# A kernel's last dense layer by seven block products instead of eight

## The chip, the core and the metric

One core of a Trainium2 chip runs the kernel. Its engines are TensorE (PE, with its weight loads as PEld), VectorE (DVE), ScalarE (ACT), GpSimd (POOL) and SyncE (SP, which here only issues DMAs). Time is device microseconds (us) for one execution.

## What is computed

Three blocks follow each other: attention with a decaying mask, a gated convolution between two dense layers, and a Fourier mix with a two-layer perceptron. The last part, cut to what the change touches (2304 tokens, 512 features, 2048 inner features):

```python
X = np.fft.fft(x, axis=1)
X = np.fft.fft(X, axis=2)
u = x + np.real(X)
mu = np.mean(u, axis=-1, keepdims=True)
var = np.mean((u - mu) ** 2, axis=-1, keepdims=True)
un = (u - mu) / np.sqrt(var + 1e-06)
ch = np.maximum(un @ w_ch1, 0.0) @ w_ch2
return u + ch
```

Inputs are float32, but the weights come as float64 and are decoded on the chip. Matmuls run on a rounded 32-bit type; every operand is split into a high and a low part, and each product is made of three matmuls (high by high, low by high, high by low; `HL` in line 46).

## The kernel before

The program records every operation with its tiles. A planner then orders them: it knows a cost for each operation and a lag between engines, walks the graph from the back for priorities and from the front for the order, and keeps the best of 40 rounds (`Plan.order`). Every engine then runs its own list strictly in order. So an edit of the recorded operations changes the lists of all engines, also far from the edit.

Up to about 460 us the lists hold attention, the gated convolution (`b_chunk`, `c_chunk`) and most of the Fourier stage (`dft`). In their gaps the weights of 7 of the 16 feature blocks (NST, 128 inner features each) are decoded (`fetch_ch`: an ACT, a POOL and three DVE operations) and put aside in DRAM; the other nine are decoded in the last stage.

The last stage is the two dense layers. Tokens go in chunks of 512, 512, 512, 512 and 256 (`chunks`, line 1081). For a chunk, `prep_u` reads the centred rows from DRAM, transposes them and splits them into high and low, into one half of `u_all` (name bc_wi in the trace), so that two chunks have room. For a chunk and a feature block:

- `ch1` (line 1110): 12 matmuls (4 slices of 128 features, three each) with 512 token columns into one of two PSUM banks (psc_c__4737 and psc_c__4738). ACT writes relu as the high part, and DVE's SCALAR_TENSOR_TENSOR the low part (bc_xs).
- `ch2` (line 1137), one block behind: for each 128 tokens three matmuls of 512 columns into an accumulator bank that stays open over all the blocks of a pass. Six banks rotate (psc_c__4989 to 4992, psdft_x__3932 and 3933).

Chunks 0 and 1 take their 16 blocks in two passes of 8, the others in one (`passes`). After the last block of a pass a 128-token tile is scaled by its 1/sqrt(var + 1e-6), computed by nine small DVE operations for each tile (`rsqrt`), added to its u row and stored. While the first passes run, the last pieces of the Fourier stage (`gens[3]`) are put between.

## Time and profile before

| | us |
|---|---|
| median of 3 runs | 866.22 (864.75 to 867.55) |
| the profiled execution's own time | 865.78 |
| its span, first to last instruction | 864.0 |
| PE busy in the span | 835.4 (97%), 5148 matmuls |
| DVE busy | 519.0 (60%) |
| ACT busy | 374.6 (43%) |
| POOL busy | 221.7 (26%) |
| mean granted clock of TensorE | 0.993 of 2.4 GHz |

Busy time of PE is that of overlapping, pipelined matmuls: the mean duration of one (some 390 ns for 512 columns) is longer than the step from one to the next. The step is read from the chain of waits, where twelve matmuls in a row have one entry. All names that begin with psc_c are PSUM banks of the last stage; a line number of 513 or 511 is that of the helper that issues every operation, so tiles tell more than lines.

### The profile page before, as it was taken

How to read it: one execution, taken by the hardware profiler on the slowest of the kernel's cores; microseconds unless marked ns; L12 is line 12 of the kernel's file. 1: busy time of each engine (PE TensorE's matmuls, PEld its weight loads, DVE VectorE, ACT ScalarE, POOL GpSimd, SP SyncE). 2: the span in 40 equal slices, each digit the busy share in tenths (PEclk: the TensorE clock that was granted, in tenths of full speed). 3: DMA queues.
4: the chain of work that ended last, by engine and by line, in shares of the span. 5: the costliest groups of instructions: out<-in, count | busy, mean ns of one | idle time of the engine just before them, and what ended most of it. 6: DMA issues, size and time to landing. Idle time of an engine off the chain costs nothing.

```text
span 864.0 us, 14103 instructions
## 1 busy us (share of the span) xinstructions
PE 835.4 (97%) x5148; PEld 703.4 (81%) x5148; DVE 519.0 (60%) x1364; ACT 374.6 (43%) x906; POOL 221.7 (26%) x252
## 2 busy tenths in 40 slices
PE   8988999899989999998999999999999999999998
PEld 6666887599878898997987888888888888888897
DVE  6978899856997374187586888676353113411141
ACT  5987798835756463274344443332121111110111
POOL 2243435401351042278465522220000000000000
PEclk9999999999999999999999999999999999999999
DMA  6454465899437414784998385433121001100110
GB/s 222 151 202 144 139 221 167 280 302 316 136 118 250 146 30 115 240 280 121 269 242 204 112 209 164 151 121 98 50 73 49 1 1 49 50 1 1 48 50 25
DMA packets 75269, 119.86 MB, mean 139 GB/s; under 512 B 10392, under 2 KB 44984, under 8 KB 75200
## 3 DMA queue, kind: packets, MB, share of 16 engines
q1 hardware_dynamic: 74624, 116.01, 44.2%
q0 software_dynamic: 576, 2.95, 1.0%
q8 instruction: 40, 0.66, 0.3%
q14 instruction: 29, 0.24, 0.1%
HBM read 93.66 MB, written 27.70 MB: 140 GB/s over the span
## 4 chain that ended last, share of the span: by engine, by line
PE 51%; DMA 4%; POOL 3%; DVE 2%; ACT 1%; issue 1%; SPq 0%; DVEq 0%; POOLq 0%; ACTq 0%
PE psc_c__4738 L513 11%; PE psc_c__4737 L513 11%; PE psc_c__4989 L513 5%; PE psc_c__4990 L513 4%; PE psdft_x__3933 L513 4%; PE psdft_x__3932 L513 4%; PE psc_c__4991 L513 3%; PE psc_c__4992 L513 3%; PE psbc_bc__537 L513 2%; PE psbc_bc__538 L513 2%; DMA dft_zz__3771<-dram_t__348 1%; POOL dft_t__3766 L513 1%; DMA dram_t__350<-glu_t__140 1%; DVE glu_cv__158 L513 1%; PE psatt_u__174 L505 1%
## 5 line engine op out<-in xcount | busy, mean ns | idle before, releaser
L513 DVE SCALAR_TENSOR_TENSOR bc_xs__131<-psc_c__4738,bc_xs__131 128x512 fp32r<-128x512 f32 (+1 forms) x40 | 25.5, 637 | 100.1 <-ACT bc_xs__131 L513 100.1
L513 DVE SCALAR_TENSOR_TENSOR bc_xs__131<-psc_c__4737,bc_xs__131 128x512 fp32r<-128x512 f32 (+1 forms) x40 | 25.4, 636 | 100.2 <-ACT bc_xs__131 L513 100.1
L513 ACT ACTIVATE bc_xs__131<-psc_c__4738 128x512 fp32r<-128x512 f32 (+1 forms) x40 | 22.2, 556 | 133.3 <-PE psc_c__4738 L513 129.2
L513 ACT ACTIVATE bc_xs__131<-psc_c__4737 128x512 fp32r<-128x512 f32 (+1 forms) x40 | 22.3, 557 | 129.6 <-PE psc_c__4737 L513 128.9
L513 PE MATMUL psbc_bc__538<-bc_xs__131,bc_wi__130 128*128 128x288 f32 x384 | 62.1, 299 | 0.0
L513 PE MATMUL psbc_bc__537<-bc_xs__131,bc_wi__130 128*128 128x288 f32 x384 | 61.7, 300 | 0.2 <-ACT glu_t__138 L513 0.2
L513 PEld LDWEIGHTS psbc_bc__537<-bc_xs__131,bc_wi__130 128*128 128x128 f32 x384 | 53.4, 188 | 1.5 <-issue 0.5
L513 PEld LDWEIGHTS psbc_bc__538<-bc_xs__131,bc_wi__130 128*128 128x128 f32 x384 | 54.0, 188 | 0.7 <-issue 0.7
L513 DVE SCALAR_TENSOR_TENSOR glu_cv__157<-glu_t__138,bc_t__132,glu_cv__157 128x576 f32<-128x576 f32 x32 | 34.4, 1076 | 12.4 <-ACT glu_cv__157 L513 12.1
L513 POOL TENSOR_SCALAR wprep_dw__125<-wprep_dw__125 128x512 f32<-128x512 f32 x24 | 16.1, 672 | 71.3 <-ACT wprep_dw__125 L513 71.0
L513 DVE SCALAR_TENSOR_TENSOR glu_cv__158<-glu_t__139,bc_t__132,glu_cv__158 128x576 f32<-128x576 f32 x32 | 32.0, 999 | 3.5 <-ACT glu_cv__158 L513 3.3
L513 DVE COPY glu_t__140<-psbc_bc__538 128x256 f32<-128x256 f32 (+2 forms) x48 | 10.0, 260 | 30.2 <-PE psbc_bc__538 L513 29.0
L513 POOL TENSOR_SCALAR wprep_dw__122<-wprep_dw__122 128x512 f32<-128x512 f32 x24 | 15.8, 656 | 43.9 <-ACT wprep_dw__122 L513 43.8
L505 PE MATMUL psatt_s__171<-att_t__67,att_t__66 64*128 64x288 f32 (+2 forms) x48 | 26.5, 553 | 0.3 <-DVE att_t__67 L513 0.3
L505 PE MATMUL psatt_s__170<-att_t__67,att_t__66 64*128 64x288 f32 (+2 forms) x48 | 26.3, 549 | 0.0
L505 PE MATMUL psatt_u__174<-att_pt__101,att_tv__92 128*64 128x448 f32 (+3 forms) x80 | 21.6, 417 | 0.6 <-ACT att_pt__102 L513 0.5
L505 PE MATMUL psatt_u__174<-att_pt__102,att_tv__93 128*64 128x448 f32 (+3 forms) x80 | 21.6, 417 | 0.0
L505 PE MATMUL psatt_s__172<-att_t__67,att_t__66 64*128 64x288 f32 (+2 forms) x48 | 21.5, 454 | 0.0
L505 PE MATMUL psatt_s__173<-att_t__67,att_t__66 64*128 64x288 f32 (+2 forms) x48 | 21.3, 449 | 0.0
L505 PE MATMUL psatt_u__169<-att_pt__101,att_tv__99 128*64 128x448 f32 (+4 forms) x72 | 19.4, 415 | 1.6 <-ACT att_pt__102 L513 1.6
L505 PE MATMUL psatt_s__170<-att_qk__70 64*128 64x288 f32 (+2 forms) x48 | 18.8, 476 | 1.8 <-DVE att_nb__95 L513 1.8
L513 DVE SCALAR_TENSOR_TENSOR wprep_dw__125<-wprep_dr__124,wprep_dw__125 128x512 int32<-128x512 int32 x24 | 20.1, 837 | 0.2
(721 smaller groups left out, 2703.1 us busy)
## 6 DMA issues: line engine op xcount, KB each, us to landing
bc_wo__133<-dram_t__346 SPq DMA_DIRECT2D x16, 512.0 KB
wprep_dr__124<-in_moe_w_ch_dram SPq DMA_DIRECT2D x16, 512.0 KB
wprep_dr__121<-in_moe_w_ch_dram SPq DMA_DIRECT2D x16, 512.0 KB
bc_wo__134<-dram_t__346 SPq DMA_DIRECT2D x16, 512.0 KB
att_qk__70<-in_qk_dram SPq DMA_DIRECT2D x8, 608.0 KB
att_qk__91<-in_qk_dram SPq DMA_DIRECT2D x8, 608.0 KB
att_rb__68<-dram_t__345 SPq DMA_DIRECT2D x32, 144.0 KB
wprep_dr__124<-in_moe_w_out_dram SPq DMA_DIRECT2D x8, 512.0 KB
```

Source lines behind the costliest of these rows:

```text
L505: getattr(eng[op.eng], f)(**{k: v.real() if isinstance(v, View) else v for k, v in kw.items()})
L513: getattr(eng[op.eng], op.fn)(**kw)
```

## The change

The first dense layer is no longer computed block by block. Two feature blocks (a pair), two halves of the 512 input features and two halves of a chunk's tokens make a 2 by 2 by 2 block product, and that is formed from seven products instead of eight: sums and differences of the blocks of the weights (`load_pair`) and of the rows (`prep_u`) are multiplied, and the seven results are added up in seven VectorE additions (`ch1`). One product is 6 matmuls with half a chunk's columns. Chunks are 512, 512, 640 and 640 tokens, so the products have 256 or 320 columns. All chunks take their 8 pairs in two passes; the first three pairs of chunks 0 and 1 are still computed the plain way. The first pass of a chunk is scaled by ACT and stored to DRAM (`y_d`), and the second adds it. `u_all` now holds one chunk (seven operands of the rows), so it is rebuilt in place at five changes of chunk. NST is 10, the weights of the last six blocks are decoded in the third and fourth pass, and `rsqrt` works on all tiles of a chunk at once.

```diff
 NH = B * H
 NT = B * S
 NP = NH // 2
-NWO, NST, NUC = 2, 7, 2
-NZT, NZR, NPQ, NUN = 1, 1, 0, 2
+NWO, NST = 2, 10
+NZT, NZR, NPQ, NUN, NUS = 1, 1, 0, 2, 1
 NZS = 1
-CUTS = (0, 8, 16)
-NMR, G3 = 7, (2, 2)
-ULE, W2E = 'V', 'V'
+G3 = 3
 NCV, NZZ, NZO, NX = 2, 4, 2, 5
 NUO, NWARM = 1, 10
 LASTW = 256
...
+    chunks = [(0, 512), (512, 512), (1024, 640), (1664, 640)]
+    passes = [(0, (0, 1, 2)), (1, (0, 1, 2)), (2, (0, 1, 2, 3, 4)), (3, (0, 1, 2, 3, 4)),
+              (3, (5, 6, 7)), (2, (5, 6, 7)), (1, (3, 4, 5, 6, 7)), (0, (3, 4, 5, 6, 7))]
+    u_all = shared[0]
-    chunks = [(512 * i, 512) for i in range(4)] + [(2048, 256)]
-    passes = [(i, range(a, z)) for a, z in zip(CUTS, CUTS[1:]) for i in (0, 1)] + [(i, range(NFC)) for i in (2, 3, 4)]
...
+    def load_pair(q, k):
+        p, w = slots[k]
+        plain = q < 3
+        wa, wb = stored(0, 2 * q), stored(0, 2 * q + 1)
+        s12, s4 = (wp.tile([128, 512], F32, tag="de", bufs=2) for _ in range(2))
+        V.tensor_tensor(out=s12[:, 0:256], in0=wb[:, 0:256], in1=wb[:, 256:512], op=ALU.add)
+        V.tensor_tensor(out=s12[:, 256:512], in0=s12[:, 0:256], in1=wa[:, 0:256], op=ALU.subtract)
+        V.tensor_tensor(out=wb[:, 0:256], in0=wa[:, 0:256], in1=wb[:, 0:256], op=ALU.subtract)
+        V.tensor_tensor(out=s4[:, 0:256], in0=wa[:, 256:512], in1=s12[:, 256:512], op=ALU.subtract)
+        if plain:
+            hi(p[1][:, 0, 0], wb[:, 0:256])
+            lo(G, p[1][:, 0, 1], wb[:, 0:256], p[1][:, 0, 0])
+        for dst, src in zip(p, (wa, wb, s12)):
+            if plain and src is not s12:
+                continue
+            hi(dst[:, :, 0], src.group(2))
+            lo(G, dst[:, :, 1], src.group(2), dst[:, :, 0])
+        hi(p[3][:, 0], s4[:, 0:256])
+        lo(G, p[3][:, 1], s4[:, 0:256], p[3][:, 0])
+        for x in range(0 if plain else 2):
+            t = stored(1, 2 * q + x)
+            hi(w[x][:, 0], t)
+            lo(V, w[x][:, 1], t, w[x][:, 0])
+
+    def u_op(n, k, j, x):
+        h = n // 2
+        if n > 512 and k == 6:
+            return u_last.over(2 * h * j + h * x, [1, h])
+        return u_all.over(4 * h * k + 2 * h * j + h * x, [1, h])
...
+    def prep_u(ci, uc):
         n = chunks[ci][1]
-        ps = ps_c1.tile([128, 512], F32, tag="c1", bufs=2)
-        k = 0
-        for d in range(4):
-            for wx, ux in HL:
-                mm(ps[:, 0:n], w1[fo][:, wx, 128 * d:128 * d + 128], U[ux][d][:, 0:n], k == 0, k == 11)
...
+        h = n // 2
+
+        def both(k, j, src):
+            up, dn = (u_op(n, k, j, x) for x in range(2))
+            hi(up, src)
+            lo(V, dn, src, up)
+
+        def wide(k, j, src):
+            up, dn = (u_all.over(4 * h * k + 2 * h * j + h * x, [4 * h, 2], [1, h]) for x in range(2))
+            hi(up, src[:, 0:n].group(2))
+            lo(V, dn, src[:, 0:n].group(2), up)
+
+        for j in range(2):
+            both(0, j, uc[j][:, 0:h])
+        for j in range(2):
+            wide(2, j, uc[j + 2])
+        for j in range(2):
+            b1, b2 = uc[j], uc[j + 2]
+            t12 = ml.tile([128, 640], F32, tag="ta")
+            V.tensor_tensor(out=t12[:, 0:h], in0=b1[:, h:n], in1=b1[:, 0:h], op=ALU.subtract)
+            V.tensor_tensor(out=t12[:, h:n], in0=b2[:, h:n], in1=t12[:, 0:h], op=ALU.subtract)
+            V.tensor_tensor(out=b1[:, h:n], in0=b2[:, h:n], in1=b1[:, h:n], op=ALU.subtract)
+            V.tensor_tensor(out=b2[:, 0:h], in0=b2[:, 0:h], in1=t12[:, h:n], op=ALU.subtract)
+            wide(4, j, t12)
+            both(1, j, b1[:, h:n])
...
+    def ch1(ci, k):
+        n = chunks[ci][1]
+        h = n // 2
+        p = slots[k][0]
+        ga_, gb_ = g_tile(n), g_tile(n)
+        a, c, d, e = (tmp.over(320 * i, [1, h]) for i in range(4))
+
+        def product(w, k):
+            ps = ps_c1.tile([128, 512], F32, tag="c1", bufs=2)[:, 0:h]
+            i = 0
+            for j in range(2):
+                for wx, ux in HL:
+                    mm(ps, w[:, wx, 128 * j:128 * j + 128], u_op(n, k, j, ux), i == 0, i == 5)
+                    i += 1
+            return ps
+
+        def gated(g, c0, v):
+            split(g[:, 0, c0:c0 + h], g[:, 1, c0:c0 + h], v)
+
+        def plus(o, ps, v):
+            V.tensor_tensor(out=o, in0=ps, in1=v, op=ALU.add)
+
+        A.activation(out=a, in_=product(p[0][:, 0], 0), func=AF.Copy)
+        plus(e, product(p[0][:, 1], 2), a)
+        gated(ga_, 0, e)
+        plus(c, product(p[2][:, 1], 5), a)
+        plus(d, product(p[1][:, 0], 1), c)
+        x = product(p[2][:, 0], 4)
+        plus(c, x, c)
+        plus(a, x, d)
+        gated(gb_, h, a)
+        plus(d, product(p[1][:, 1], 6), d)
+        gated(gb_, 0, d)
+        plus(c, product(p[3], 3), c)
+        gated(ga_, h, c)
+        return ga_, gb_
+
...
+    def ch2(step):
+        ci, k, gs, acc, first, last, final, end = step
         t0, n = chunks[ci]
-        gh, gl = g_
-        first, last = fo == fos[0], fo == fos[-1]
+        if last:
...
+            for f in range(2):
+                g, w = gs[f], slots[k][1][f]
+                for i, (gx, wx) in enumerate(HL):
+                    mm(acc[t], g[:, wx, 128 * t:128 * t + 128], w[:, gx], first and f == 0 and i == 0, last and f == 1 and i == 2)
             if last:
                 r = t0 + 128 * t
-                ut = ml.tile([128, 514], F32, tag="ut", bufs=2)
-                dma(out=ut, in_=Flat(u_d, UW * r, [UW, 128], [1, UW]))
-                rstd = rsqrt(ut[:, 513:514])
-                if fo == NFC - 1:
-                    V.tensor_scalar(out=ut[:, 0:512], in0=ut[:, 0:512], scalar1=ut[:, 512:513], scalar2=None, op0=ALU.add)
-                cols = 512 if ci + 1 < len(chunks) else LASTW
+                if not final:
+                    ut = mr.tile([128, 512], F32, tag="us", bufs=NUS)
+                    A.activation(out=ut, in_=acc[t], func=AF.Copy, scale=rstd[:, t:t + 1])
+                    dma(out=y_d[r:r + 128], in_=ut)
+                    continue
+                ut, yt = wp.tile([128, 512], F32, tag="dw", bufs=2), ml.tile([128, 512], F32, tag="yt", bufs=1)
+                dma(out=ut, in_=Flat(u_d, UW * r, [UW, 128], [1, DM]))
+                dma(out=yt, in_=y_d[r:r + 128])
+                V.scalar_tensor_tensor(out=ut, in0=ut, scalar=st[:, t, 0:1], in1=yt, op0=ALU.add, op1=ALU.add)
+                cols = LASTW if end else 512
                 for c in range(0, 512, cols):
                     o = ut[:, c:c + cols]
-                    V.scalar_tensor_tensor(out=o, in0=acc[t][:, c:c + cols], scalar=rstd, in1=o,
+                    V.scalar_tensor_tensor(out=o, in0=acc[t][:, c:c + cols], scalar=rstd[:, t:t + 1], in1=o,
                                            op0=ALU.mult, op1=ALU.add)
-                    dma(out=out[r:r + 128, c:c + cols] if fo == NFC - 1 else Flat(u_d, UW * r + c, [UW, 128], [1, cols]), in_=o)
-
-    pend = None
-    for k, (ci, fos) in enumerate(passes):
-        if ci not in us:
-            us[ci] = prep_u(ci)
-        acc = {}
-        for fo in fos:
-            for _ in range(G3[k] if k < len(G3) else 0):
-                next(gens[3], None)
-            if fo not in w1:
-                w1[fo] = load_ch(0, fo, G)
-                w2[fo] = load_ch(1, fo, G if W2E == 'G' else V)
-            g_ = ch1(ci, fo, us[ci])
-            if pend:
-                ch2(*pend)
-            pend = (ci, fos, fo, g_, acc)
-    ch2(*pend)
+                    dma(out=out[r:r + 128, c:c + cols], in_=o)
...
+    todo = [(w, fo) for fo in range(NST, NFC) for w in range(2)]
+
+    def decode_some(m):
+        for _ in range(m):
+            if todo:
+                w, fo = todo.pop(0)
+                dma(out=wch_d[2 * fo + w], in_=fetch_ch(w, fo))
+
+    pend, acc, home = None, {}, {}
+    prep_plain(0)
+    load_plain(0, 0)
+    prep_plain(1)
+    flat = [(i, ci, q) for i, (ci, qs) in enumerate(passes) for q in qs]
+    for i, (pi, ci, q) in enumerate(flat):
+        qs = passes[pi][1]
+        if q == qs[0]:
+            acc = {}
+            if pi in (2, 3, 5, 6, 7):
+                prep_u(ci, turned)
+            if pi in (2, 4, 5, 6):
+                turned = turn_u(passes[pi + 1][0])
+        for _ in range(G3):
+            next(gens[3], None)
+        k = q % 5
+        if pi == 0 and q < 2:
+            load_plain(q + 1, q + 1)
+        gs = plain_ch1(ci, k) if pi < 2 else ch1(ci, k)
+        if pend:
+            ch2(pend)
+        pend = (ci, k, gs, acc, q == qs[0], q == qs[-1], pi > 3, pi + 1 == len(passes))
+        if pi == 1:
+            load_pair(q, k)
+            if q == qs[0]:
+                turned = turn_u(2)
+        if pi == 2:
+            decode_some(2)
+            if q < 2:
+                load_pair(q + 3, q + 3)
+        if pi == 3:
+            decode_some(2)
+            if 0 < q < 4:
+                load_pair(q + 4, q - 1)
+    ch2(pend)
```

TensorE, well inside the last stage. Before, one feature block of a 512-token chunk (psc_c_0__4737 is the first layer's bank, the four names after it are accumulators of the second layer):

```order
L513 MATMUL psc_c_0__4737<-bc_wi__130,ml_t_0__5271 128x512 x12
L513 MATMUL psc_c_0__4989<-ml_t_0__5270,bc_xs__131 128x512 x3
L513 MATMUL psc_c_0__4990<-ml_t_0__5270,bc_xs__131 128x512 x3
L513 MATMUL psc_c_0__4991<-ml_t_0__5270,bc_xs__131 128x512 x3
L513 MATMUL psc_c_0__4992<-ml_t_0__5270,bc_xs__131 128x512 x3
L513 MATMUL psc_c_1__4738<-bc_wi__130,ml_t_0__5273 128x512 x12
```

Now a pair of a 640-token chunk from its first product on (psc_c_0__4873 and psc_c_1__4874 are the first layer's two banks, ml_t_0__5372 to 5375 the weight sums of the pair, the rest accumulators):

```order
L511 MATMUL psc_c_0__4873<-bc_wi__130,ml_t_0__5372 128x320 x6
L511 MATMUL psc_c_1__4874<-bc_wi__130,ml_t_0__5372 128x320 x6
L511 MATMUL psdft_x__3869<-mr_t_0__4899,ml_t_0__5371 128x512 x3
L511 MATMUL psc_c_0__4873<-bc_wi__130,ml_t_0__5374 128x320 x6
L511 MATMUL psc_c_0__5045<-mr_t_0__4904,bc_xs__131 128x512
L511 MATMUL psc_c_1__4874<-bc_wi__130,ml_t_0__5373 128x320 x6
L511 MATMUL psc_c_0__5045<-mr_t_0__4904,bc_xs__131 128x512 x2
L511 MATMUL psc_c_0__4873<-bc_wi__130,ml_t_0__5374 128x320 x6
L511 MATMUL psc_c_0__5045<-mr_t_0__4905,bc_xs__131 128x512
L511 MATMUL psc_c_1__4874<-ml_t_0__5370,ml_t_0__5373 128x320 x6
L511 MATMUL psc_c_0__5045<-mr_t_0__4905,bc_xs__131 128x512 x2
L511 MATMUL psc_c_0__5046<-mr_t_0__4904,bc_xs__131 128x512
```

A bank used to be filled by 12 long matmuls and then left alone for 12 of the second layer; it is now filled by 6 shorter ones, and the other bank's next product follows at once or after one to three matmuls of the second layer.

TensorE at the change from chunk 2 to chunk 3 in the changed kernel. The rows on ml_t_0__5379 to 5381 are the old chunk's last products (ml_t_0__5370 and bc_wi__130 hold the rows' operands), that on bc_xs__131 with 128x320 the new chunk's first:

```order
L511 MATMUL psc_c_1__4874<-ml_t_0__5370,ml_t_0__5379 128x320 x6
L511 MATMUL psc_c_0__5044<-ml_t_0__5377,bc_xs__131 128x512 x2
L511 MATMUL psc_c_0__5046<-ml_t_0__5382,bc_xs__131 128x512 x3
L511 MATMUL psc_c_0__5047<-ml_t_0__5382,bc_xs__131 128x512
L511 MATMUL psc_c_0__4873<-bc_wi__130,ml_t_0__5381 128x320 x6
L511 MATMUL psc_c_0__5047<-ml_t_0__5382,bc_xs__131 128x512 x2
L511 MATMUL psc_c_1__4874<-bc_wi__130,bc_xs__131 128x320 x6
L511 MATMUL psc_c_0__5046<-ml_t_0__5383,ml_t_0__5371 128x512 x2
L511 MATMUL psc_c_0__5047<-ml_t_0__5383,ml_t_0__5371 128x512 x2
L511 MATMUL psc_c_0__5046<-ml_t_0__5383,ml_t_0__5371 128x512
L511 MATMUL psc_c_0__5047<-ml_t_0__5383,ml_t_0__5371 128x512
L511 MATMUL psc_c_1__4874<-bc_wi__130,mr_t_0__4892 128x320 x3
```

Between the old chunk's last product (the fifth row) and the new chunk's first (the seventh) stand two matmuls of the second layer. Before, the next chunk's rows had a half of bc_wi of their own.

VectorE, in the same part of the program. Before, at the change from one chunk to the next (the rows on wprep_de and bc_wi build the next chunk's rows, those on psc_c_0__4737 and psc_c_1__4738 empty the first layer's banks, those on ml_ut finish an output tile):

```order
L513 STREAM_TRANSPOSE wprep_de__123<-bc_xs__131 128x512
L513 TENSOR_TENSOR bc_wi__130<-wprep_de__126,bc_wi__130 128x512
L513 TENSOR_TENSOR bc_wi__130<-wprep_de__123,bc_wi__130 128x512
L513 SCALAR_TENSOR_TENSOR bc_xs__131<-psc_c_0__4737,bc_xs__131 128x512
L513 SCALAR_TENSOR_TENSOR ml_ut__5255<-psc_c_0__4991,ml_rs_0__5256,ml_ut__5255 128x512
L513 SCALAR_TENSOR_TENSOR ml_ut__5259<-psc_c_0__4992,ml_rs_1__5260,ml_ut__5259 128x512
L513 STREAM_TRANSPOSE wprep_de__126<-bc_xs__131 128x512
L513 SCALAR_TENSOR_TENSOR bc_xs__131<-psc_c_1__4738,bc_xs__131 128x512
```

Now, in the first pass of a 640-token chunk (ml_t_0__5369 holds the partial sums, wprep_dw, de and dr the decoding of a weight block):

```order
L511 TENSOR_SCALAR wprep_de__126<-wprep_dw__125 128x512
L511 TENSOR_TENSOR ml_t_0__5369<-psc_c_0__4873,ml_t_0__5369 128x320
L511 SCALAR_TENSOR_TENSOR wprep_dw__125<-wprep_dr__124,wprep_de__126 128x512
L511 TENSOR_SCALAR wprep_de__123<-wprep_dw__122 128x512
L511 SCALAR_TENSOR_TENSOR ml_t_0__5371<-ml_t_0__5369,ml_t_0__5371 128x320
L511 SCALAR_TENSOR_TENSOR wprep_dw__122<-wprep_dr__121,wprep_de__123 128x512
L511 SCALAR_TENSOR_TENSOR bc_xs__131<-ml_t_0__5369,bc_xs__131 128x320
L511 SCALAR_TENSOR_TENSOR wprep_dw__122<-wprep_dr__121,wprep_dw__122 128x512
L511 SCALAR_TENSOR_TENSOR wprep_dw__125<-wprep_dr__124,wprep_dw__125 128x512
L511 TENSOR_TENSOR ml_t_0__5369<-psc_c_0__4873,ml_t_0__5369 128x320
L511 TENSOR_TENSOR ml_t_0__5369<-psc_c_1__4874,ml_t_0__5369 128x320
```

A product's result is now added by a VectorE operation that stands in one list with the decoding of weights: here five decoding operations of 512 elements and two low parts of 320 lie between two additions that read the same bank.

## Rows read from the trace of the kernel before

**Rows 1.** The page: span and part 1, busy us, share of span, instructions.

```profile
span 864.0 us, 14103 instructions
...
PE 835.4 (97%) x5148; PEld 703.4 (81%) x5148; DVE 519.0 (60%) x1364; ACT 374.6 (43%) x906; POOL 221.7 (26%) x252
```

**Rows 2.** Busy time by stretch (us): PE, PEld, DVE, ACT, POOL, PEclk, DMA, GB/s.

```profile
0.00:460.00 460.00, 436.38 (x3299) 374.01 (x3300) 336.99 (x866) 288.54 (x756) 179.90 (x197) 0.99 0.63 195
460.00:864.00 404.00, 399.00 (x1851) 329.39 (x1849) 182.02 (x500) 86.08 (x150) 41.78 (x55) 1.00 0.26 75
...
480.00:540.00 60.00, 60.00 (x274) 49.57 (x273) 50.83 (x126) 23.93 (x40) 20.72 (x28) 1.00 0.58 164
540.00:812.00 272.00, 272.00 (x1179) 220.97 (x1178) 99.97 (x279) 46.32 (x78) 10.21 (x13) 1.00 0.17 51
812.00:864.00 52.00, 48.17 (x304) 43.16 (x302) 16.82 (x64) 6.16 (x16) 0.00 (x0) 0.99 0.16 51
```

**Rows 3.** The chain that ended last: start us, us, engine, tile, matmuls.

```profile
348.53 1.60 PE psbc_bc__537 L513 x12
...
546.47 2.80 PE psc_c__4737 L513 x12
...
554.83 0.70 PE psc_c__4991 L513 x3
...
646.81 2.72 PE psc_c__4737 L513 x12
...
816.95 1.43 PE psc_c__4738 L513 x12
...
847.75 1.39 PE psc_c__4737 L513 x12
```

**Rows 4.** VectorE groups by shape, 460 to 864 us: busy, mean ns, idle before.

```profile
L513 DVE SCALAR_TENSOR_TENSOR bc_xs__131<-psc_c__4738,bc_xs__131 128x512 fp32r<-128x512 f32 x31 | 21.4, 689 | 81.8 <-ACT bc_xs__131 L513 81.8
...
L513 DVE SCALAR_TENSOR_TENSOR bc_xs__131<-psc_c__4738,bc_xs__131 128x256 fp32r<-128x256 f32 x8 | 3.4, 425 | 14.6 <-ACT bc_xs__131 L513 14.6
...
L513 DVE TENSOR_TENSOR bc_wi__130<-wprep_de__126,bc_wi__130 128x256 fp32r<-128x256 f32 x2 | 0.8, 404 | 2.4 <-ACT bc_wi__130 L513 2.4
...
L513 DVE SCALAR_TENSOR_TENSOR wprep_dw__122<-wprep_dr__121,wprep_de__123 128x512 int32<-128x512 int32 x9 | 6.2, 689 | 0.2
...
L513 DVE TENSOR_SCALAR wprep_de__123<-wprep_dw__122 128x512 int32<-128x512 int32 x9 | 4.1, 456 | 0.6 <-POOL wprep_dw__122 L513 0.6
...
L513 DVE SCALAR_TENSOR_TENSOR ml_rs__5257<-ml_rs__5256,ml_rs__5258 128x1 f32<-128x1 f32 x39 | 10.5, 270 | 0.3
...
L513 DVE STREAM_TRANSPOSE wprep_de__123<-bc_xs__131 128x256 f32<-128x256 f32 x2 | 0.8, 424 | 0.0
```

**Rows 5.** VectorE groups by shape, whole span, two that read a PSUM bank.

```profile
L513 DVE TENSOR_TENSOR dft_ue__3779<-dft_zr__3778,psdft_x__3933 128x257 f32<-128x257 f32 x4 | 1.6, 404 | 0.0
...
L513 DVE TENSOR_TENSOR att_xr__108<-psatt_u__174,att_rb__68 128x448 f32<-128x448 f32 x8 | 5.0, 622 | 5.1 <-PE psatt_u__174 L505 3.5 <-ACT bc_wi__130 L513 1.2 <-ACT att_t__79 L513 0.3
```

**Rows 6.** Timeline around 821 us: start us, us, engine, instruction, idle before.

```profile
821.03 0.87 PE L513 MATMUL psc_c__4989<-bc_wo__134,bc_xs__131 128*128 128x512 f32 x3
821.24 0.39 ACT L513 ACTIVATE bc_xs__131<-psc_c__4737 128x256 fp32r<-128x256 f32 x1 [2.44 <-PE psc_c__4737 L513]
...
821.65 0.42 DVE L513 SCALAR_TENSOR_TENSOR bc_xs__131<-psc_c__4737,bc_xs__131 128x256 fp32r<-128x256 f32 x1 [2.40 <-ACT bc_xs__131 L513]
```

**Rows 7.** Timeline of SyncE's queue: a store, and the next load into its tile.

```profile
826.36 0.34 SPq L513 DMA_DIRECT2D out_dram<-ml_ut__5255  x1
...
828.39 0.33 SPq L513 DMA_DIRECT2D ml_ut__5255<-dram_t__351  x1
```

**Rows 8.** Busy time by stretch, three stretches in which TensorE waited.

```profile
50.00:100.00 50.00, 46.42 (x362) 35.94 (x361) 41.43 (x130) 38.58 (x111) 19.76 (x19) 0.97 0.51 159
150.00:200.00 50.00, 46.72 (x367) 37.01 (x366) 36.20 (x114) 30.58 (x93) 13.08 (x15) 1.00 0.87 290
400.00:420.00 20.00, 16.36 (x111) 15.02 (x111) 12.50 (x27) 7.43 (x16) 11.76 (x17) 0.91 0.86 225
```

More of the change, by code (lines that the diff above doesn't have):

```diff
@@ L588, in build @@
     u_d = dram.tile([NT, UW], F32)
-    wch_d = [dram.tile([128, 512], F32) for _ in range(2 * NST)]
+    y_d = dram.tile([NT, DM], F32)
+    wch_d = [dram.tile([128, 512], F32) for _ in range(2 * NFC)]
     dd_d = dram.tile([128, 2, 1284], F32R)
@@ L850, in go @@
                 u = 2 * c + part
-                if half == 0:
+                if half == 0 and b == B - 1:
+                    for i in {0: range(6), 3: (6,), 4: (7,)}.get(u, ()):
+                        load_wo(i)
+                elif half == 0:
                     if u == 0:
@@ L888, in bc_chunks @@
         return out_
-    queue = []
+    queue, shared = [], []
     def bc_step():
@@ new lines, in build @@
+    passes = [(0, (0, 1, 2)), (1, (0, 1, 2)), (2, (0, 1, 2, 3, 4)), (3, (0, 1, 2, 3, 4)),
+              (3, (5, 6, 7)), (2, (5, 6, 7)), (1, (3, 4, 5, 6, 7)), (0, (3, 4, 5, 6, 7))]
+    u_all = shared[0]
+    rest = bc.tile([128, 5760], F32R, tag="xs")
+    small = bc.tile([128, 24], F32, tag="cw")
+    tmp = ml.tile([128, 4 * 320], F32)
+    u_last = ml.tile([128, 1280], F32R)
+    g_last = ml.tile([128, 1280], F32R)
+    st, rs = small.over(0, [2, 5], [1, 2]), [small.over(10 + 5 * k, [1, 5]) for k in range(2)]
@@ new lines, in quad, with pair @@
+    def quad(pool):
+        return pool.tile([128, 2, 2, 256], F32R)
+    def pair(pool):
+        return pool.tile([128, 2, 512], F32R)
+    slots = []
+    for k in range(5):
+        pool = mr if k < 3 else ml
+        if k:
+            p = [quad(pool) for _ in range(3)] + [pool.tile([128, 2, 256], F32R)]
+        else:
+            p = [rest.over(4096, [512, 2], [256, 2], [1, 256]),
+                 bc.tile([128, 2, 2, 256], F32R, tag="wo", bufs=NWO), quad(pool),
+                 rest.over(5120, [256, 2], [1, 256])]
+        w = [pair(pool) if k or x else bc.tile([128, 2, 512], F32R, tag="wo", bufs=NWO) for x in range(2)]
+        slots.append((p, w))
@@ new lines, in u_op, with fetch_u @@
+    def u_op(n, k, j, x):
[3 more added lines that the diff above has]
+        return u_all.over(4 * h * k + 2 * h * j + h * x, [1, h])
+    def fetch_u(t0, m):
+        ux = wp.tile([128, 1024], F32, tag="dr", bufs=2)
+        for k in range(4):
+            dma(out=ux[32 * k:32 * k + 32].over(0, [128, m // 32], [1, 128]),
+                in_=Flat(u_d, UW * t0 + 128 * k, [UW, 32], [32 * UW, m // 32], [1, 128]))
+        return ux
@@ new lines, in turn_u @@
+    def turn_u(ci):
+        t0, n = chunks[ci]
+        uc = {}
+        for d in (0, 2, 1, 3):
+            uc[d] = ml.tile([128, 640], F32, tag="uc", bufs=4)
+        for a in range(0, n, 256):
+            m = min(256, n - a)
+            ux = fetch_u(t0 + a, m)
+            for d in (0, 2, 1, 3):
+                V.transpose(out=uc[d][:, a:a + m], in_=ux.over(32 * d, [128, m // 32], [1, 32]))
+        return uc
+    def prep_u(ci, uc):
+        n = chunks[ci][1]
+        h = n // 2
[20 more added lines that the diff above has]
+            both(1, j, b1[:, h:n])
+            both(6, j, b2[:, 0:h])
@@ L1141, in ch2 @@
         for t in range(n // 128):
             if first:
-                k = turn[0] % 6
-                turn[0] += 1
-                acc[t] = ps_c2.tile([128, 512], F32, tag=f"c{k}") if k < 4 else bank3()
-            for k, (gx, wx) in enumerate(((gh, 0), (gl, 0), (gh, 1))):
-                mm(acc[t], gx[:, 128 * t:128 * t + 128], w2[fo][:, wx], first and k == 0, last and k == 2)
+                b = turns[0] % 6
+                turns[0] += 1
+                acc[t] = ps_c2.tile([128, 512], F32, tag=f"c{b}") if b < 4 else bank3()
```

123 lines of the change are left out of this document (66 added, 57 removed).

## The prediction

> **What bounds the kernel now.** I read four views in this order.
>
> The windows by stretch come first [rows 2]. From 460 to 864 us TensorE is busy 399.00 of 404 us, and from 540 to 812 us all of 272.00 of 272 us, at granted clock 1.00. VectorE is busy 182.02 us there and ScalarE 86.08. So in the last stage the time is that of the matmuls, and a matmul less shortens the span by its own step. Before 460 us TensorE misses 23.6 us in many small waits.
>
> The chain of waits then gives that step, the time from one matmul to the next, since their busy times overlap [rows 3]. Twelve matmuls of 512 columns take 2.80 and 2.72 us in the first and last of 52 such pieces (mean 2.78, so 0.2317 us each). Twelve of 256 columns take 1.43 and 1.39 us in the first and last of 16 (mean 1.41, 0.1173 us each).
>
> Third, VectorE's groups by shape give the price of what the change puts on it [rows 4, 5]. Last, the timeline shows how a bank is emptied [rows 6] and how a store holds its tile [rows 7].
>
> The sum is made against the profiled execution's own 865.78 us (span 864.0 [rows 1] and 1.8 around it). The median of the runs is 0.4 us higher, which is added at the end.
>
> **TensorE, what goes.** Before, the first dense layer has 4 chunks x 16 blocks x 12 = 768 matmuls of 512 columns and 16 x 12 = 192 of 256: 768 x 0.2317 + 192 x 0.1173 = 177.9 + 22.5 = 200.4 us.
>
> After, there are three kinds. The plain part is 6 blocks x 2 chunks x 12 = 144 of 512 columns, 33.4 us. The block products of chunks 0 and 1 are 10 pairs x 7 x 6 = 420 of 256, 49.2 us. Those of chunks 2 and 3 are 16 pairs x 7 x 6 = 672 of 320. No row has 320 columns. Pro rata of the 512-column step they take 0.1448 us, of the 256-column step 0.1466; the nearest row of another width, 1.60 us for twelve of 288 [rows 3], gives 0.148. I take 0.146, so 98.1 us (97.3 to 99.5). The sum is 180.7 us, so TensorE saves 19.7 us (18.3 to 20.5). The second layer keeps its 864 matmuls of 512 columns.
>
> There are 276 more matmuls, and as many weight loads. Weight loads average 329.39 / 1849 = 178 ns in the last stage [rows 2], more than a 256-column step, so they could set the step. They don't in the last chunk of before, where 192 matmuls of 256 columns, each with its own load, sustain 0.117 us. I charge nothing.
>
> **VectorE, what comes.** A pair needs seven additions that read a PSUM bank, and four low parts. An addition reading a bank takes 404 ns at 257 columns and 622 at 448 [rows 5], as from the other memory (404 at 256 [rows 4]), so 0.48 us at 320. Low parts take 425 and 689 ns at 256 and 512 [rows 4], so 0.49 at 320. A pair costs 7 x 0.404 + 4 x 0.425 = 4.5 us at 256 columns and 7 x 0.48 + 4 x 0.49 = 5.3 at 320. TensorE spends on the same pair 42 x 0.1173 + 24 x 0.2317 = 10.5 us and 42 x 0.146 + 30 x 0.2317 = 13.1 us. So VectorE keeps up on average.
>
> For the whole last stage I count: evacuation +87 us (10 x 4.5 + 16 x 5.3 + 12 x 0.69, less 64 x 0.69 + 16 x 0.43 before, rounded), rows +51 (three rebuilds of 10.0 us, worked out below, two of 8.4, 12 transposes of 640 and 8 of 512 at 0.424 us for 256 [rows 4], less 15.5 for three chunks before), weight sums +13 (8 pairs x 4 x 0.404), the 1/sqrt work -25 (an estimate: 26 tiles with six operations of 0.27 us [rows 4] and three shorter ones, against 8 chunk passes with twelve), decoding -11 (12 blocks for 18, each 2 x 0.689 + 0.456 = 1.83 us [rows 4]). That is 182 + 115, about 300 us, in a stage of some 385: 78%, where it was 45%. In the first pass of the first 640-token chunk it is denser: five pairs 26.5, ten decodings (five steps of two) 18.3, two loads of a weight pair 6, transposing and rebuilding the other chunk's rows, or most of it, 10: about 61 of TensorE's 65 us.
>
> **The wait this can make.** Two banks take turns. A bank's turnaround is now ScalarE or VectorE alone: after the product's end 0.21 us pass, then 0.39 to 0.42 us of work [rows 6], and about 0.2 us back; that is 0.8 to 0.9 us. The other bank's product covers 6 x 0.1173 = 0.70 us (256 columns) or 0.88 (320), and matmuls of the second layer, three of which take 0.70 us [rows 3], lie between: 24 or 30 of them for each seven products. So an addition must be over 0.7 us late to stop TensorE, and one decoding operation of 0.689 us ahead of it nearly is that. Per product the wait is bounded by nothing and by 0.15 us (the mean if one in five waits out one such operation). I take 0.022 us x 182 products = 4 us.
>
> **The change of chunk.** Rows had two halves of `u_all`; now they are rebuilt in place, five times. The transposes are done ahead into their own tiles. After the last reader of an operand VectorE does at 320 columns six low parts of 320 and four of 640, and eight sums: 6 x 0.48 + 4 x 0.82 + 8 x 0.48 = 10.0 us. The products of the next chunk begin two matmuls of the second layer behind the old one's last, but an operand is rebuilt as soon as its own product is done: between the last use of the first operand and its next lie five products and some 23 other matmuls, 9.7 us. TensorE has at hand, for the rest, the last pair's products, 6.1 us, and two pairs of the second layer, 13.9 us: 20 us against VectorE's 10.0 plus two pairs of its own, 10.6. That is balanced, so the stall lies between 0 and 3 us at each. I take 0.6, the end that the order's long cover is nearer to: 5 x 0.6 = 3 us.
>
> **Edits that cost nothing, and what covers them.** A first pass is stored to DRAM through one tile: ScalarE's 0.66 us and a store held until the next use, 2.03 us from a store to the next load of its tile [rows 7], so 2.9 us a tile. A 640-token pass holds five of six accumulator banks, so the new pass has one free and needs the next after 6 matmuls; the 6.1 us of the next pair's products and its position one pair behind cover it. Without that cover it is 1 to 2 us at each of six passes. Three more blocks decoded before 460 us are 6 x 1.83 = 11 us more of VectorE, where it is busy 336.99 of 460 [rows 2]; they go into gaps, 0 to 2 us, taken as 0. Waiting at the end, 52.00 - 48.17 = 3.8 us [rows 2], stays.
>
> **Sum.** 865.8 - 19.7 + 4 + 3 = 853.1, and 0.4 for the median: 853.5 us.
>
> **Rivals.**
> 1. All is hidden: nothing is given back, 846.5 us. For it speaks VectorE's 78% on average; against it that its 61 of 65 us leave no slack in one stretch.
> 2. Every change of chunk stalls 3 us: 15 us in place of 3 is 12 more, 861.5 without the evacuation's part and 865.5 with it. A VectorE that is late at the change is late for the products too, so these are mostly the same microseconds: 862. For it speaks that 20 stands against 20.6 us.
> 3. The clock. Where TensorE waited in small pieces, its granted clock was 0.97 (50 to 100 us) and 0.91 (400 to 420 us), but also 1.00 with as much waiting (150 to 200 us) [rows 8]. The two levels are 1.2 and 2.4 GHz, so 0.97 is a mean of both. At 0.97 over a stage of 385 us the loss is 11.6 us: 865. The granted clock of 1.00 over 272 us with no wait speaks against it as long as products queue without gaps. The Trainium skill ("TensorE: Matmul & The Clock Gate", "A second HAM failure mode: psum-queue depth-cycling") says that a TensorE that is busy on average but drains its queue whenever a bank is emptied can have its clock fall and rise in turn; more frequent hand-overs of two banks are of that kind. By that rule it would be this rival, without it the forecast; the trace bears it out in one of two like stretches.
> 4. The slower side: VectorE's list. An addition stands behind decodings, transposes and row sums, with five decoding operations between two additions that read the same bank. TensorE then waits per product on VectorE. The gain is gone at 19.7 / 182 = 0.108 us a product; at 0.15, the changes of chunk in it, it is 27.3 us: 865.8 - 19.7 + 27.3 + 0.4 = 873.8 us. For it speaks the dense stretch; against it that other stretches have VectorE at half load.
>
> **How the numbers follow.** The forecast, 848 to 858 by its own terms, has 0.62; rival 1 0.08, rival 2 0.16, rival 3 0.05, rival 4 0.09. The measurement tells 0.3% (2.6 us) from no change: faster is below 863.6, slower above 868.8. Faster holds the forecast, rival 1 and most of rival 2 (0.11): 0.81, taken as 0.80. Within are the rest of rival 2, rival 3 and the milder part of rival 4: 0.10. Slower is the rest, 0.10. The range runs from just under rival 1, 845.5, to 864.5, so that rival 4 and half of rival 3 are left out.
>
> **What would show it.** Right: products of 320 columns take 0.88 us and of 256 0.70 in the chain, TensorE's busy time falls by about 20 us, VectorE is near 300 us in the last stage at clock 1.00, and TensorE's idle time there is 7 us, half at the five changes of chunk. Wrong: idle time of tens of us released by VectorE on psc_c banks (rival 4), stalls of 3 us released by writes to bc_wi (rival 2), a granted clock under 0.99 after 460 us (rival 3), or a step of 320 columns near 0.18 us, which would put the weight loads in charge: 672 x 0.034 = 23 us, and the gain gone.

## The result, and the profile after

The changed kernel is slower, not faster: 870.98 us median of 10 runs (867.74 to 873.19) against 865.63 (864.25 to 867.55), ratio 1.0061 (95% interval 1.0046 to 1.0077). The forecast was 853.5 and its range ended at 864.5. The profiled execution took 873.15 us. So the medians lie 5.4 us apart, and the profiled executions, from which the rows below come, 7.4.

The page of the changed kernel, its span and part 1, answers to [rows 1]:

```profile
span 871.4 us, 15330 instructions
...
PE 828.5 (95%) x5424; PEld 719.2 (83%) x5424; DVE 652.9 (75%) x1596; ACT 430.2 (49%) x1043; POOL 250.7 (29%) x271
```

TensorE works 6.9 us less (835.4 before), VectorE 134 us more. The windows by stretch answer to [rows 2] (columns as there):

```profile
0.00:460.00 460.00, 424.63 (x3156) 361.75 (x3157) 343.05 (x876) 285.03 (x746) 177.69 (x189) 0.97 0.64 196
460.00:872.00 412.00, 403.86 (x2270) 357.41 (x2269) 309.90 (x720) 145.21 (x298) 73.06 (x82) 1.00 0.43 120
540.00:812.00 272.00, 269.66 (x1523) 241.65 (x1522) 217.62 (x511) 100.20 (x210) 37.86 (x35) 1.00 0.41 116
```

From 540 to 812 us TensorE is busy 269.66 of 272 at granted clock 1.00, as it was. But up to 460 us it has done 3156 matmuls, where it had done 3299 [rows 2]. The chain of waits answers to [rows 3]: a product of 320 columns, one of 256, and the two places at which VectorE held TensorE up (start, us, what):

```profile
545.78 0.88 PE psc_c__4873 L511 x6
...
573.15 1.45 DVE wprep_de__126 L511
...
687.94 1.28 DVE ml_ta__5388 L511
...
762.87 0.71 PE psc_c__4874 L511 x6
```

Where the time went shows in two rows of TensorE's timeline for each kernel, the first matmul into a first-layer bank and the last matmul of the program (start, us, engine, instruction). Before:

```profile
444.39 0.62 PE L513 MATMUL psc_c__4737<-bc_wi__130,m_t__3759 128*128 128x512 f32 x2
...
859.32 0.85 PE L513 MATMUL psc_c__4990<-ml_t__5278,bc_xs__131 128*128 128x512 f32 x3
```

After:

```profile
470.34 0.62 PE L511 MATMUL psc_c__4874<-bc_wi__130,bc_wo__133 128*128 128x512 f32 x2
...
866.63 0.84 PE L511 MATMUL psdft_x__3869<-mr_t__4905,bc_xs__131 128*128 128x512 f32 x3
```

The last stage lasted 859.32 + 0.85 - 444.39 = 415.8 us and now lasts 866.63 + 0.84 - 470.34 = 397.1: 18.7 less. It begins 26.0 us later. Together that is +7.3, nearly all of the 7.4 by which the span grew. The windows, cut at the start of the stage (before, then after):

```profile
0.00:444.39 444.39, 421.01 (x3209) 361.00 (x3209) 326.26 (x845) 282.40 (x745) 167.11 (x182) 0.99 0.62 194
444.39:864.00 419.61, 414.36 (x1942) 342.41 (x1940) 192.75 (x520) 92.22 (x162) 54.57 (x71) 1.00 0.28 80
```

```profile
0.00:470.34 470.34, 434.97 (x3232) 371.95 (x3233) 349.82 (x891) 288.81 (x754) 180.24 (x194) 0.97 0.64 195
470.34:871.40 401.06, 393.52 (x2194) 347.21 (x2192) 303.13 (x706) 141.43 (x289) 70.51 (x78) 1.00 0.43 119
```

In the stage TensorE's busy time falls by 20.8 us, as forecast. Ahead of it, for nearly the same matmuls (3209 and 3232), TensorE is idle 12.0 us more (35.4 for 23.4) and busy 14.0 us more, at a granted clock of 0.97 for 0.99. So the change does in the last stage what was forecast, or somewhat better, and the loss lies ahead of it, in lists that compute nothing new, save for the decoding of three more blocks.

### The profile page after: what moved, and what is told of

Same layout as the page of the kernel before. It is cut to its first block, busy times and chain, and to the rows that moved or that the text cites. A ratio compares the mean times of both kernels' runs of the same rounds, so it can differ in the third digit from the quotient of the medians.

```text
span 871.4 us, 15330 instructions
## 1 busy us (share of the span) xinstructions
PE 828.5 (95%) x5424; PEld 719.2 (83%) x5424; DVE 652.9 (75%) x1596; ACT 430.2 (49%) x1043; POOL 250.7 (29%) x271
## 4 chain that ended last, share of the span: by engine, by line
PE 66%; DVE 15%; DMA 6%; ACT 6%; issue 3%; POOL 3%; SPq 1%; DVEq 0%; ACTq 0%; POOLq 0%
PE psc_c__4874 L511 9%; PE psc_c__4873 L511 9%; PE psbc_bc__556 L511 6%; PE psbc_bc__557 L511 6%; PE psdft_x__3869 L511 4%; PE psdft_x__3870 L511 4%; PE psc_c__5047 L511 4%; PE psc_c__5046 L511 3%; PE psc_c__5045 L511 3%; PE psc_c__5044 L511 3%; DVE glu_cv__158 L511 3%; PE psatt_s__170 L503 3%; DVE glu_cv__157 L511 3%; PE psatt_u__174 L503 2%; PE psatt_u__174 L511 2%
## 5 line engine op out<-in xcount | busy, mean ns | idle before, releaser
L511 ACT ACTIVATE bc_xs__131<-ml_t__5369 128x320 fp32r<-128x320 f32 (+1 forms) x78 | 35.1, 450 | 98.4 <-DVE ml_t__5369 L511 87.3
L511 DVE TENSOR_TENSOR ml_t__5369<-psc_c__4874,ml_t__5369 128x320 f32<-128x320 f32 (+1 forms) x91 | 40.9, 461 | 26.2 <-PE psc_c__4874 L511 25.2
L511 DVE TENSOR_TENSOR ml_t__5369<-psc_c__4873,ml_t__5369 128x320 f32<-128x320 f32 (+1 forms) x91 | 41.0, 461 | 25.4 <-PE psc_c__4873 L511 23.0
L511 POOL TENSOR_SCALAR wprep_dw__125<-wprep_dw__125 128x512 f32<-128x512 f32 x24 | 17.9, 748 | 104.5 <-ACT wprep_dw__125 L511 104.4
L511 DVE SCALAR_TENSOR_TENSOR bc_xs__131<-ml_t__5369,bc_xs__131 128x320 fp32r<-128x320 f32 (+1 forms) x78 | 38.8, 499 | 10.6 <-ACT bc_xs__131 L511 10.2
L511 POOL TENSOR_SCALAR wprep_dw__122<-wprep_dw__122 128x512 f32<-128x512 f32 x24 | 16.6, 691 | 73.2 <-ACT wprep_dw__122 L511 73.1
L511 DVE COPY glu_t__140<-psbc_bc__557 128x256 f32<-128x256 f32 (+2 forms) x48 | 9.9, 261 | 35.4 <-PE psbc_bc__557 L511 31.9
L511 DVE SCALAR_TENSOR_TENSOR glu_cv__157<-glu_t__138,bc_cw__132,glu_cv__157 128x576 f32<-128x576 f32 x32 | 32.7, 1021 | 1.4 <-ACT glu_cv__157 L511 1.2
L511 DVE SCALAR_TENSOR_TENSOR glu_cv__158<-glu_t__139,bc_cw__132,glu_cv__158 128x576 f32<-128x576 f32 x32 | 31.3, 979 | 2.8 <-ACT glu_cv__158 L511 2.7
L511 ACT ACTIVATE glu_t__140<-psbc_bc__556 128x256 f32<-128x256 f32 (+2 forms) x48 | 8.5, 251 | 45.6 <-PE psbc_bc__556 L511 40.8
L511 ACT ACTIVATE ml_t__5371<-ml_t__5369 128x320 fp32r<-128x320 f32 (+1 forms) x26 | 11.7, 449 | 35.1 <-DVE ml_t__5369 L511 29.0
```

What stands on the lines that cost most here:

```text
L511: getattr(eng[op.eng], op.fn)(**kw)
```

## The experiments

Three theories were tested. The change also puts two tiles of the Fourier stage into rings of other tiles to win space: the last token tile of a sequence (`zt32`) into the four slots of `zz`, and a small low part (`al`) into the one slot of `zr`. Either these rings hold the work back (buffers), or the three blocks more that are decoded early do (decode), or the planner drew other lists for the first 460 us (order). Each ratio is to the kernel before, with its 95% interval.

**Own buffers for the two tiles**, 852.28 us, 0.9833 (0.9810 to 0.9857):

```diff
-                al = dp.tile([33, 512], F32R, tag="zr", bufs=NZR)
+                al = dp.tile([33, 512], F32R, tag="abl", bufs=1)
-            zt = dp.tile([128, 16, w], F32, tag=f"zt{w}" if w > 32 else "zz", bufs=NZT if w > 32 else NZZ)
+            zt = dp.tile([128, 16, w], F32, tag=f"zt{w}", bufs=NZT)
```

> The changed kernel, but in the Fourier stage the last token tile (zt32) and the small low part (abl) have buffers of their own again, as before the change, in place of a turn in the rings zz and zr. Buffer theory (the last stage gives its 19.7 us, and the shared rings hold back the Fourier stage and so the start of the last stage): 855 to 862, with the last matmul into psbc some 10 us earlier than at 468.5 us. Decode theory (three more blocks decoded early cost the front): 868 to 873, as the changed kernel. Order theory (any change of the recorded program gives the planner other lists for the first 460 us, good or bad by chance): anywhere from 855 to 875, with no link to the rings.

That is within 1.3 us of the forecast. Its timeline, the same two rows:

```profile
449.04 0.62 PE L511 MATMUL psc_c__4838<-bc_wi__130,bc_xs__131 128*128 128x512 f32 x2
...
845.38 0.84 PE L511 MATMUL psdft_x__3988<-mr_t__4868,bc_xs__131 128*128 128x512 f32 x3
```

The stage lasts 397.2 us as in the changed kernel, and begins 21.3 us earlier.

**The kernel before with the two tiles in rings** (the same edit the other way), 890.49 us, 1.0282 (1.0254 to 1.0310):

> The kernel before, with these two buffers put into the rings zz and zr and nothing else changed. Buffer theory: 872 to 882, the start of the last stage 8 to 15 us later than at 444 us. Decode theory: 865.6, no change. Order theory: anywhere from 858 to 880.

It loses more than the theory had. Its stage begins 9.5 us later (first matmul at 453.87) and lasts 11.5 us longer; what makes the second part is open. In neither of the two edits does the number of blocks decoded early change, so decoding makes neither difference. The next two tried it by itself.

**Seven blocks decoded early, in the changed kernel**, 871.70 us, 1.0068 (1.0044 to 1.0092), and **ten in the kernel before** (NST alone, the other way), 872.04 us, 1.0061 (1.0040 to 1.0082):

```diff
-NWO, NST = 2, 10
+NWO, NST = 2, 7
-            decode_some(2)
+            decode_some(3)
```

> The changed kernel with seven blocks decoded early in place of ten; the other nine are decoded in the third and fourth pass. Decode theory: the front gets its time back, 858 to 864, if the last stage hides the six more decodings of 1.83 us. Buffer theory: 869 to 877, the front as late as it was and VectorE denser in the third pass. Order theory: anywhere from 860 to 880.

> The kernel before with ten blocks decoded early in place of seven, and nothing else changed. Decode theory: 872 to 880. Buffer theory: 865 to 867, hidden in gaps of the first 460 us. Order theory: anywhere from 860 to 878.

The first gains nothing in all: its stage begins 12.1 us earlier (458.29), but lasts 407.5 us, 10.4 longer, so the last stage doesn't hide six more decodings. The second is 6.4 us slower and its stage begins 8.7 us later (453.05), which alone would speak for decoding; the orders below show that an order by itself moves this kernel by more. What three blocks more cost the front is therefore not shown.

**The changed kernel's own lists, with own buffers**, 870.66 us, 1.0058 (1.0035 to 1.0081). The program is recorded twice and the second is issued in the order planned for the first. The order was planned for several slots of the token tile, so some sequences' last tokens are computed from another sequence's tile.

```diff
+def build(*args):
+    rings, own = record(True, *args), record(False, *args)
+    rings.analyse()
+    own.emit(rings.order())
```

> The changed kernel's program in exactly its own order on every engine, but the last token tile and the small low part lie in buffers of their own, so that only the waits for the rings are gone. Wait theory (instructions stand still for a ring's slot): most of the 18.7 us between the changed kernel (871.0) and the one with own buffers (852.3) come back, 853 to 860. Order theory (the planner, told of the rings, writes other lists for the first 460 us, and these cost the time whatever the buffers do): 866 to 872.

With the rings' waits gone (but for those of the token tile's one slot) and the lists kept, the time stays. So it is mainly the lists that cost the 18.7 us, and not instructions that stand still for a ring's slot. Windows of the changed kernel, then of the one with own buffers, bear this out from 100 to 200 us, up to 350 us, and (for own buffers; the changed kernel's stands above) up to the start of the stage:

```profile
100.00:200.00 100.00, 88.90 (x681) 71.88 (x680) 79.05 (x238) 67.49 (x194) 35.28 (x34) 0.95 0.68 218
0.00:350.00 350.00, 325.20 (x2452) 268.87 (x2453) 277.48 (x745) 238.75 (x646) 116.86 (x127) 0.97 0.59 187
```

```profile
100.00:200.00 100.00, 95.30 (x769) 77.78 (x770) 82.03 (x259) 75.63 (x221) 34.76 (x34) 1.00 0.69 232
0.00:350.00 350.00, 327.84 (x2504) 272.01 (x2505) 275.69 (x748) 238.59 (x649) 119.17 (x127) 0.99 0.60 192
0.00:449.04 449.04, 423.72 (x3223) 363.26 (x3224) 341.91 (x872) 286.93 (x753) 178.56 (x191) 0.99 0.66 203
```

From 100 to 200 us TensorE is busy 6.4 us less, at a granted clock of 0.95 against 1.00, and the first load into a ring is issued only at 358.39 us:

```profile
358.39 0.42 SPq L511 DMA_DIRECT2D dft_zz__3766<-dram_t__341  x1
```

At 350 us the changed kernel is 52 matmuls behind, some 7 us at 2504 in 350 us: a third of the 21.3 us by which its stage begins later. The other two thirds arise where the rings are in use, and there the run with the kept lists is the evidence. Up to the start of the stage the changed kernel's TensorE is idle some 10 us more than with own buffers and busy some 11 us more, at a granted clock of 0.97 for 0.99.

From 100 to 200 us one wait of the changed kernel stands out (who waited for whom: us, times, longest). It returns in the run with its lists and own buffers, and not with the other lists:

```profile
PE psbc_bc__556 L511 <- DMA bc_wo__134<-dram_t__340: 5.1, 1, 5.1
```

```profile
PE psbc_bc__556 L510 <- DMA bc_wo__134<-dram_t__340: 4.9, 1, 4.9
```

**One tile at a time**: the low part alone in a buffer of its own 858.34 us, 0.9912 (0.9890 to 0.9933); the token tile alone 850.66 us, 0.9822 (0.9801 to 0.9843); and in the kernel before the token tile alone in its ring 876.81 us, 1.0122 (1.0106 to 1.0138). Each edit is one of the two lines above.

> The changed kernel with a buffer of its own for the small low part (abl) alone; the last token tile stays in the ring zz. If the token tile is the one that costs (it holds one of the four input tiles of the next sequence until its sequence's last step): 867 to 873. If the low part is (its DMA copy holds the one slot of zr that every row step needs): 852 to 858. If each has a part: between.

> The changed kernel with a buffer of its own for the last token tile (zt32) alone; the low part stays in the ring zr. If the token tile is the one that costs: 851 to 858. If the low part is: 867 to 873. If each has a part: between.

> The kernel before with the last token tile (zt32) alone in the ring zz; the low part keeps its buffer. Both in rings cost this kernel 24.4 us (890.5). If the token tile is the one that costs: 880 to 892. If it needs both, as the changed kernel's 858.3 with the token tile alone in the ring against 871.0 with both says: 870 to 880. If the low part is the one: 864 to 868.

Taking either tile out of its ring gives back most, so the parts don't add up: 12.6 and 20.3 us against 18.7 for both. In the kernel before, the token tile alone costs 11.1 us against 24.4 for both. A choice among orders could look like that, and it was tried next.

**Other orders of the same programs.** The planner makes 40 orders and keeps the one whose time it estimates lowest. One line takes another:

```diff
-            if best is None or span < best[0]:
+            if k == 27:
```

> The changed kernel with the lists of another of the planner's 40 rounds (27 in place of 18, whose lists it holds to be just as good). If the rings bind every order (ring theory): 868 to 875, the last matmul into psbc near 468 us again. If the changed kernel only drew a bad order by chance (chance theory): 852 to 862 is as likely as 871.

> The same with a third order of the changed kernel (round 20), which the planner holds to be nearly as good. Ring theory: 868 to 876. Chance theory: at least one of the two other orders is over 6 us away from 871.

> The kernel before with the lists of the planner's second best round (17 in place of 29), nothing else changed: how far the choice of an order alone moves this program. Ring theory: 864 to 870, a spread of a few us that is small beside the 18.7 between shared and own buffers. Chance theory: 855 to 885, as far from 865.6 as the ring variants are.

> The kernel before in the planner's third best order (round 25). If the order that the kernel before holds is a lucky one of its kind: 870 to 878, as round 17 (874.2). If round 17 is an unlucky one: 862 to 868.

> The changed kernel with both buffers of its own, in the planner's second best order of it (round 18 in place of 15). If the rings cost 8 us or more in any order: 850 to 858, below both other orders of the changed kernel (860.1, 861.3). If own buffers only drew a good order: 858 to 866, as those.

> The same in the third best order (round 16). If the rings cost 8 us or more in any order: 850 to 858. If own buffers only drew a good order: 858 to 866.

> The kernel before with both buffers in the rings, in another order (round 12 in place of 29). If the rings cost the kernel before 10 to 15 us and the rest of the 24.4 us was the order: 875 to 885. If they cost 20 and more: 886 to 895.

| program | order kept | another | a third | middle |
|---|---|---|---|---|
| before | 865.6 | 874.2, 1.0101 (1.0083 to 1.0118) | 874.5, 1.0102 (1.0081 to 1.0123) | 874.2 |
| before, rings | 890.5 | 892.2, 1.0301 (1.0280 to 1.0321) | | 891.4 |
| changed (rings) | 871.0 | 860.1, 0.9937 (0.9925 to 0.9949) | 861.3, 0.9948 (0.9934 to 0.9962) | 861.3 |
| changed, own buffers | 852.3 | 856.4, 0.9885 (0.9866 to 0.9904) | 845.3, 0.9758 (0.9738 to 0.9778) | 852.3 |

Ring theory and order theory are both half right. All three orders with rings are slower than all three without, and in the kernel before both are slower than all three. And the order alone is worth 8.9 us in the kernel before and 10.9 in the changed one. The middle values make one account of it: the kernel before holds an order 8.6 us better than its middle, the change with own buffers gains 21.9, the rings cost 9.0, and the changed kernel holds an order 9.7 worse than its middle: 865.6 + 8.6 - 21.9 + 9.0 + 9.7 = 871.0. It closes by the way it is made, so it is no proof of its terms: column by column the rings cost 18.7, 3.7 and 16.0 us, and three orders a program can't say more than "some 10 us".

The start of the stage, read as above from each kernel's timeline, moves in the same way. In the columns' order it is 444.4, 454.6 and 456.4 us before, 470.3, 460.1 and 456.3 with the rings, 449.0, 453.1 and 442.4 with own buffers. The starts of the kernels with another number of blocks decoded early (453.1 before, 458.3 with rings, 446.9 with own buffers, the last from a run below) lie inside these spreads.

The third order with own buffers, 845.26 us, is the fastest version found. Its two rows:

```profile
442.35 0.62 PE L511 MATMUL psc_c__4838<-bc_wi__130,bc_xs__131 128*128 128x512 f32 x2
...
838.85 0.84 PE L511 MATMUL psdft_x__3988<-mr_t__4868,bc_xs__131 128*128 128x512 f32 x3
```

Its stage lasts 397.3 us again, and only the start moved. The same two rows of the changed kernel in round 27, a stage of 394.0 us that begins 10.3 us earlier than in the order it holds:

```profile
460.05 0.62 PE L511 MATMUL psc_c__4889<-bc_wi__130,bc_xs__131 128*128 128x512 f32 x2
...
853.16 0.84 PE L511 MATMUL psdft_x__3829<-mr_t__4928,bc_xs__131 128*128 128x512 f32 x3
```

**Own buffers and seven blocks early**, 860.28 us, 0.9935 (0.9912 to 0.9959); both edits above:

> The changed kernel with both buffers of its own and seven blocks decoded early in place of ten, the other nine in the third and fourth pass. If the three blocks cost the first 460 us what they cost the kernel before (6.4 us, 872.0 against 865.6) and the last stage hides them: 845 to 848. If the last stage, where VectorE is busy 299 of 390 us, can't hide 11 us more in its third and fourth pass: 852 to 860. If neither place notices: 850 to 854.

It is the second case, just above its range: the stage begins 2.1 us earlier than with ten blocks (446.95) and lasts 407.5 us, 10.4 longer. TensorE's longest waits from 480 us on, and the windows of the stretch with the decodings, first this kernel and then the one with ten blocks:

```profile
PE psc_c__4817 L511 <- DVE ml_t__5304 L511: 4.7, 4, 1.9
```

```profile
560.00:720.00 160.00, 152.50 (x807) 134.48 (x807) 123.49 (x265) 61.74 (x123) 29.64 (x31) 0.98 0.44 133
```

```profile
560.00:720.00 160.00, 159.25 (x876) 142.79 (x875) 127.97 (x281) 63.88 (x130) 27.38 (x26) 1.00 0.41 120
```

With 18 decodings in place of 12, VectorE is late for the additions, TensorE does 69 matmuls fewer in 160 us and its granted clock is 0.98 for 1.00. This is the fourth rival, in the size that six more decodings give it.

## Why the prediction was wrong

**The step that failed** is "Edits that cost nothing, and what covers them". It priced the three blocks decoded early at 0 and took the work up to 460 us as otherwise unchanged, so the sum has no term for the start of the last stage. That start moved by 26.0 us. The runs show two things in it: two tiles in rings (9.0 us between the middle values), which the prediction did not price at all, and the order that each kernel happened to hold (8.6 and 9.7 us between kept and middle). These sizes rest on three orders a program. That an edit at the end rewrites the lists of the first 460 us was known, and was given no term and no range. Of the four rivals none has it: the slower side came by a mechanism that was not named, while the additions that were to make it (the fourth) cost 2.3 us.

**TensorE, what goes: right.** Products of six matmuls take 0.88 and 0.71 us in the chain, 0.147 and 0.118 us a matmul against 0.146 and 0.1173. No weight load sets the step. The stage is 18.7 us shorter, where the sum had 19.7 less 7.

**The wait, and the change of chunk: mis-sized, both too large.** TensorE waits for VectorE's additions twice:

```profile
PE psc_c__4873 L511 <- DVE ml_t__5369 L511: 2.3, 2, 1.5
```

That is 2.3 us where 4 and 3 were taken. The first rival, everything hidden, was nearer for the stage. Of the five changes of chunk one stalls, and for an addition, not for a rebuilt operand. The wait of 1.5 us stands behind sums of weight blocks and the 1/sqrt operations (from 573.15 in the chain), the one of 0.8 behind sums of rows (687.94). Both times GpSimd was writing low parts, and several of VectorE's sums took some three times as long as by themselves:

```profile
572.89 1.42 POOL L511 TENSOR_TENSOR ml_t__5372<-wprep_dw__125,ml_t__5372 128x512 fp32r<-128x512 f32 x1 [14.89 <-ACT ml_t__5372 L511]
...
573.07 1.53 DVE L511 TENSOR_TENSOR wprep_de__126<-wprep_de__126,wprep_dw__125 128x256 f32<-128x256 f32 x1
...
686.56 0.42 DVE L511 TENSOR_TENSOR wprep_de__126<-wprep_de__126,wprep_dw__125 128x256 f32<-128x256 f32 x1
...
688.83 1.54 POOL L511 TENSOR_TENSOR mr_t__4896<-wprep_de__126,mr_t__4896 128x512 fp32r<-128x512 f32 x1
...
689.14 1.58 DVE L511 TENSOR_TENSOR ml_uc__5384<-ml_uc__5385,ml_uc__5384 128x320 f32<-128x320 f32 x1
...
690.64 0.48 DVE L511 TENSOR_TENSOR ml_t__5369<-psc_c__4873,ml_t__5369 128x320 f32<-128x320 f32 x1
...
691.17 0.85 PE L511 MATMUL psc_c__4873<-bc_wi__130,mr_t__4895 128*128 128x320 f32 x4 [0.82 <-DVE ml_t__5369 L511]
```

The prediction gave these operations one price, whatever GpSimd did. The "about 0.2 us back" in its turnaround of a bank was too long here: TensorE went on 0.05 us after the addition's end (690.64 + 0.48, then 691.17).

**VectorE, what comes: right in sum.** 309.90 us from 460 to 872 us, with some of the front's work in it, for about 300. The groups by shape, at 320 columns (busy us, mean ns, idle before):

```profile
L511 DVE TENSOR_TENSOR ml_t__5369<-psc_c__4873,ml_t__5369 128x320 f32<-128x320 f32 x56 | 26.7, 487 | 14.4 <-PE psc_c__4873 L511 13.5
...
L511 DVE SCALAR_TENSOR_TENSOR bc_xs__131<-ml_t__5369,bc_xs__131 128x320 fp32r<-128x320 f32 x48 | 26.3, 550 | 4.3 <-ACT bc_xs__131 L511 4.0
...
L511 DVE TENSOR_TENSOR bc_wi__130<-ml_uc__5386,bc_wi__130 128x320 fp32r<-128x320 f32 x6 | 3.8, 640 | 0.0
```

An addition takes 487 ns for 480 forecast, a low part 550 for 490, and the rows' low part 640 for 480. The last mean is one of two durations (last section).

**The clock: right for the stage, missed ahead of it.** From 540 to 812 us the granted clock is 1.00, while products of 0.71 and 0.88 us take turns in two banks. The Trainium skill ("TensorE: Matmul & The Clock Gate", "A second HAM failure mode: psum-queue depth-cycling") has the clock rise and fall where TensorE idles for short times between groups of matmuls. This trace doesn't put that to the test, since TensorE is busy 269.66 of these 272 us. Ahead of the stage, where it waited, as from 100 to 200 us, its granted clock was 0.95.

The forecast of 853.5 meets the own-buffer kernel (852.3) only by luck, by errors that cancel: its stage is 18.6 us shorter where 12.7 were forecast, and it begins 4.7 us later (449.04 for 444.39) where nothing was.

**Open.** Which rows of the list make the changed kernel's order bad was not isolated; the load of bc_wo that TensorE waits 5.1 us for is one candidate, argued and not tried. In the run with kept lists the token tile's one slot can bring waits of its own, so part of the time could have been exchanged rather than kept. Three orders a program are few. Two other edits ahead of the last stage (weights of the output projection loaded early, constants loaded in pieces) were not tried alone.
